# Attention with a sliding window and sinks, fed into a two-layer network: a new order for the first stretch, a third home for P, run-time numbers spread by a product

## The chip, the cores and the metric

The kernel runs on one core of a Trainium2 chip. The metric is the device time of one execution in microseconds (us), as the median of three runs. TensorE (PE in the profile; PEld is its weight load) does the matrix products. VectorE (DVE) and ScalarE (ACT) do the elementwise work, GpSimd (POOL) prepares a few constants, and SyncE (SP) issues nearly all transfers between DRAM and the core's memory. Matrix products are written to PSUM, which has eight banks of 128 x 512 floats.

## The reference

```python
def _attn_ref(q, k, v, n_sink, window):            # 4 batches, 8 heads, 768 positions, 64 wide
    scores = scale * np.matmul(q, k.transpose(0, 1, 3, 2))
    keep = (pos[None, :] < int(n_sink)) | ((rel >= 0) & (rel < int(window)))   # rel = row - column
    scores = np.where(keep, scores, -1000000000.0)
    a = np.exp(scores - np.max(scores, axis=-1, keepdims=True))
    a = a / (np.sum(a, axis=-1, keepdims=True) + 1e-09)
    return np.matmul(a, v).astype(np.float32)

def _moe_ref(x, w_in, w_out):                      # x: 3072 x 512, w_in: 512 x 2048, w_out: 2048 x 512
    h = x @ w_in
    relu6 = np.clip(h + 3.0, 0.0, 6.0)
    return ((h * relu6 / 6.0) @ w_out).astype(np.float32)
```

The attention's output, heads side by side, is the x of the second function. n_sink (4) and window (128) are 64-bit integers that reach the kernel as data, so the masks are computed on the chip. w_in and w_out are 64-bit floats, which the kernel turns into 32-bit pairs itself.

## The kernel before, in words

The work is cut into 12 units of 256 positions (one batch, one third of its sequence), and each unit into 4 pairs of heads: 48 pairs. The steps of pair s have names in a plan, which are used below:

- kq and v: transfers of K and Q, and of V. C: scores on TensorE (four products: two tiles t by two heads h). t: mask, scale and row maximum on DVE, which writes P. x: exponential on ACT, with the row sum. c: reciprocal of the sum on DVE. n: P times the reciprocal, on ACT or DVE, whichever the plan finds free. D: transposes of P on TensorE. o: copy of the transposed P on ACT. E: P times V on TensorE. xh and xl: the result split into a high part (ACT) and a rest (DVE).
- The weights come in 32 parts. Part k is loaded (w), and turned from 64-bit into a high and a low 32-bit tile by wa and wb (ACT), wc and wd (DVE), wh (either) and wl (DVE).
- For unit n and slice i (0 to 7) of the 2048 hidden columns, F (FFN1) is two halves of 12 products each, and needs the xl of the unit's four pairs and parts 4i and 4i+1. r, s, h, g are the gate between the layers (r on ACT, s and g on DVE). G (FFN2) is two halves of 6 products, and needs parts 4i+2 and 4i+3.

Pairs 0 to 11, the first third of each batch, use plain 32-bit products ("plain" in the code). The others split their operands into two rounded parts first.

The order on each engine is made before the kernel is built, by a planner (`in_order`): it keeps a clock for each engine, and gives a free engine the ready task with the earliest due time, as long as the buffers that it takes (`ROOM`) are free. Due times are numbers in tables (`PART_DUE`, `LEAD`, `AHEAD`, `LATE`, `GLAG`). The engines then run their lists strictly in that order and wait for each other by semaphores. Where TensorE has nothing ready early on, the planner writes an "idle" product of two constants (L303) into its list, up to the planned time `QUIET`. Ahead of all that stand `WARM` such products.

P of a plain pair lives in one of two homes: the buffer Pt (even pairs) or two of pl (odd pairs), and K and Q in two buffers each. Pair s+2 can't be masked before the transposes of pair s have freed the home.

n_sink and window are read by two transfers that write the numbers to all 128 partitions (L314, L315); two small DVE instructions turn them into floats (L317, L319), and five more build the masks (L332, L335).

Of the kernel before, what the change touches and what calls it, by code (L numbers as in the profile page):

```python
# [19 lines left out]
P = 128  # L20
SK = 16
# [4 lines left out]
WARM = 10  # L26
# [18 lines left out]
def all_tasks():  # L45
# [6 lines left out]
    add("mask", "DVE", 5.0, [], -100)  # L52
    for s in range(PAIRS):
# [3 lines left out]
        if f32:  # L57
            add(f"kq{s}", "SP", 0.95, [], d - LEAD["kq"], ("kq",))
            add(f"v{s}", "SP", 0.47, [], d - LEAD["v"], ("V",))
            hold = ("pl", "pl") if s % 2 else ("Pt",)  # L60
            add(f"C{s}", "PE", 1.03, [f"kq{s}"], d, ("bank",) * 4 + hold, ("kq",), 0.35)
            scores = [f"C{s}", f"C{s}"]
        else:
# [6 lines left out]
            add(f"qh{s}", "*", (0.54, 0.336), [f"qa{s}"], d - AHEAD["kt"] + 0.2, ("qt",))  # L70
# [76 lines left out]
    for n in range(UNITS):  # L147
        xs = [f"xl{4 * n + p}" for p in range(4)]
        for i in range(8):
# [4 lines left out]
            add(f"F{n}.{i}.0", "PE", 1.42, xs + before + [f"wl{4 * i}", f"wl{4 * i + 1}"], d, ("bank",))  # L154
            add(f"F{n}.{i}.1", "PE", 1.42, [f"F{n}.{i}.0"], d + 0.1, (), ("x0", "x1", "x2", "x3") if i == 7 else (), 0.25)
# [18 lines left out]
def in_order(tasks):  # L174
# [3 lines left out]
    free = dict(PE=5.5, ACT=2.9, DVE=1.0, SP=0.8)  # L178
# [11 lines left out]
    while marks:  # L190
# [9 lines left out]
        while moved:  # L200
            moved = False
            for k, e in enumerate(engines):
# [60 lines left out]
def attn_ffn_kernel(ctx: ExitStack, tc: tile.TileContext, qx, kx, vx, vfx, vsx, n_sink, window, w_in, w_out, out):  # L263
# [53 lines left out]
    nc.vector.scalar_tensor_tensor(out=neg, in0=raw[:, :, 0], scalar=0.0, in1=raw[:, :, 1], op0=ALU.is_lt, op1=ALU.add)  # L317
# [691 lines left out]
```

## Time and profile before

| what | value |
| --- | --- |
| median of 3 runs | 701.63 us (701.29 to 703.6) |
| time of the profiled execution | 702.55 us |
| its span, first to last instruction | 700.6 us |
| TensorE busy | 692.1 us, 99% |
| DVE busy, ACT busy | 559.5 us (80%), 459.1 us (66%) |
| TensorE's granted clock, mean over the span | 0.997 |
| idle products in the trace (L303) | 114 records, 17.2 us |

The span leaves out 1.95 us of the profiled execution's time, which lie around it. An fp32 product of the idle kind or of a plain pair is recorded as two matmuls, so 114 records are 57 products. Matmuls overlap in the records: what one costs is the distance from its start to the start of the next, not its own length. A TensorE that is busy 99% of the span is not doing useful work 99% of the span, since the idle products count as busy.

### The profile page before, as it was taken

The numbers are of one execution on the slowest core, as the hardware profiler recorded it, in microseconds if no ns is written. First come the engines' busy times: TensorE is split into PE (matmuls) and PEld (weight loads), VectorE is DVE, ScalarE is ACT, GpSimd is POOL, SyncE is SP. The second block draws the span as 40 slices with busy tenths as digits, with TensorE's granted clock in tenths as the row PEclk, the third lists the DMA queues.
The fourth block names the chain that finished last, engine by engine and source line by source line (L and its number), as shares of the span: only waits on it lengthen the run. The fifth ranks groups of instructions, "written<-read, shape, count | busy, mean of one in ns | idle before, by whom it ended". The sixth has DMA issues, their size and how long they took to land.

```text
span 700.6 us, 13148 instructions
## 1 busy us (share of the span) xinstructions
PE 692.1 (99%) x4792; PEld 633.2 (90%) x4792; DVE 559.5 (80%) x1396; ACT 459.1 (66%) x1167; POOL 4.5 (1%) x18
## 2 busy tenths in 40 slices
PE   9999999999999999999999999999999999999996
PEld 8888899899999999999999999999999999999995
DVE  6999997368789889889888889888989988885221
ACT  6997986565657677757676667676766776764222
POOL 2000000000000000000000000000000000000000
PEclk9999999999999999999999999999999999999998
DMA  8775562122222213232123123212321222200001
GB/s 282 238 223 183 181 196 67 61 69 78 72 81 84 67 39 92 63 88 92 51 63 118 51 62 110 72 51 80 83 79 56 76 65 75 91 3 0 31 1 36
DMA packets 40122, 61.51 MB, mean 88 GB/s; under 512 B 4720, under 2 KB 31088, under 8 KB 40048
## 3 DMA queue, kind: packets, MB, share of 16 engines
q1 hardware_dynamic: 39760, 60.57, 28.8%
q8 instruction: 40, 0.66, 0.4%
q14 instruction: 34, 0.28, 0.1%
q10 hardware_dynamic: 288, 0.00, 0.0%
HBM read 54.27 MB, written 6.29 MB: 86 GB/s over the span
## 4 chain that ended last, share of the span: by engine, by line
PE 91%; DVE 4%; ACT 3%; DMA 1%; issue 0%; ACTq 0%; POOL 0%; POOLq 0%; DVEq 0%
PE hps L732 37%; PE o L769 37%; PE av L679 6%; PE sp L542 5%; PE pt L607 3%; DMA st<-in_w_out_dram 1%; ACT Ph L569 1%; PE pt L683 1%; DVE Ph L552 1%; PE idle L303 1%; PE pt L605 1%; DMA st<-in_w_in_dram 1%; PE sp L539 1%; ACT st L390 1%; ACT wt L388 0%; DVE wt L396 0%
## 5 line engine op out<-in xcount | busy, mean ns | idle before, releaser
L732 PE MATMUL hps<-xh,wih 128*128 128x256 f32 x768 | 221.7, 289 | 0.0
L732 PE MATMUL hps<-xh,wil 128*128 128x256 f32 x768 | 217.2, 283 | 0.0
L732 PE MATMUL hps<-xl,wih 128*128 128x256 f32 x768 | 217.1, 283 | 0.0
L769 PE MATMUL o<-woh,gh 128*128 128x512 f32 (+1 forms) x386 | 153.3, 397 | 0.0
L769 PE MATMUL o<-wol,gh 128*128 128x512 f32 (+1 forms) x386 | 151.0, 391 | 0.0
L769 PE MATMUL o<-woh,g 128*128 128x512 f32 (+1 forms) x386 | 150.8, 391 | 0.0
L732 PEld LDWEIGHTS hps<-xh,wih 128*128 128x128 f32 x768 | 146.8, 191 | 2.8 <-DVE nb L552 0.3
L732 PEld LDWEIGHTS hps<-xl,wih 128*128 128x128 f32 x768 | 147.0, 191 | 2.1
L732 PEld LDWEIGHTS hps<-xh,wil 128*128 128x128 f32 x768 | 146.7, 191 | 0.0
L744 DVE SCALAR_TENSOR_TENSOR gf<-gf,hps 128x512 f32<-128x512 f32 x96 | 65.3, 680 | 36.5 <-ACT gf L741 35.9
L741 ACT ACTIVATE gf<-hps,three 128x512 f32<-128x512 f32 x96 | 65.0, 677 | 44.5 <-PE hps L732 44.4
L769 PEld LDWEIGHTS o<-woh,g 128*128 128x128 f32 x386 | 72.5, 188 | 16.4 <-DVE g L750 0.6
L769 PEld LDWEIGHTS o<-woh,gh 128*128 128x128 f32 x386 | 72.9, 189 | 11.5 <-issue 0.7
L769 PEld LDWEIGHTS o<-wol,gh 128*128 128x128 f32 x386 | 72.8, 189 | 10.4
L253 ACT ACTIVATE ph<-pm 128x512 fp32r<-128x512 f32 x61 | 38.6, 632 | 61.9 <-DVE pm L617 61.9
L569 ACT ACTIVATE Pt<-Pt,nb 128x144 f32<-128x144 f32 (+2 forms) x144 | 59.0, 411 | 28.6 <-DVE Pt L560 26.6
L750 DVE TENSOR_TENSOR g<-gf,gh 128x512 fp32r<-128x512 f32 x96 | 66.4, 691 | 11.6 <-ACT gh L253 10.2
L639 DVE TENSOR_TENSOR pl<-pm,ph 128x512 fp32r<-128x512 f32 x64 | 44.3, 691 | 35.0 <-ACT ph L253 34.9
L253 ACT ACTIVATE gh<-gf 128x512 fp32r<-128x512 f32 x66 | 41.5, 629 | 26.0 <-DVE gf L744 25.9
L552 DVE CUSTOM_DVE_ANT_0 Pt<-sp,m_t 128x272 f32<-128x272 f32 x128 | 51.4, 433 | 0.0
L542 PE MATMUL sp<-kt,qt 128*128 128x272 f32 (+2 forms) x288 | 46.9, 292 | 0.0
L617 DVE TENSOR_TENSOR pm<-pt,side 128x512 f32<-128x512 f32 x64 | 43.8, 685 | 0.5
(108 smaller groups left out, 1031.9 us busy)
## 6 DMA issues: line engine op xcount, KB each, us to landing
kd<-in_kx_dram SPq DMA_DIRECT2D x64, 200.0 KB, 3.4
qd<-in_qx_dram SPq DMA_DIRECT2D x72, 128.0 KB, 3.1
st<-in_w_in_dram SPq DMA_DIRECT2D x16, 512.0 KB, 4.7
st<-in_w_out_dram SPq DMA_DIRECT2D x16, 512.0 KB, 4.1
vr<-in_vx_dram SPq DMA_DIRECT2D x32, 192.0 KB, 2.7
out_dram<-ost SPq DMA_DIRECT2D x23, 256.0 KB, 2.0
VF<-in_vfx_dram SPq DMA_DIRECT2D x12, 256.0 KB, 4.2
kr<-in_kx_dram SPq DMA_DIRECT2D x12, 128.0 KB, 4.2
```

The costliest lines, as they stand in the source:

```text
L253: nc.scalar.mul(out=out, in_=src, mul=scale)
L542: nc.tensor.matmul(out=sp[g][:, 0:w], lhsT=d["qt"][:, i, g, ts], rhs=d["kt"][:, g, ks], start=(i == 0), stop=(i == 1))
L552: nc.vector.tensor_tensor_reduce(out=cell(s, g, t, 0, w), in0=sp[g][:, 0:w], in1=m[:, 0:w], scale=-SCALE, scalar=3.0e38, op0=ALU.add, op1= ...
L569: nc.scalar.activation(out=blk, in_=blk, func=AF.Exp, scale=-1.0, bias=d["nb"][:, i:i + 1], accum_out=d["sm"][:, i:i + 1])
L617: nc.vector.tensor_tensor(out=pm, in0=pt.unsqueeze(2).to_broadcast([P, 2, 2, P]), in1=side.unsqueeze(1).to_broadcast([P, 2, 2, P]), op=ALU ...
L639: nc.vector.tensor_tensor(out=pl[:, 0:w], in0=pt[:, 0:w], in1=ph[:, 0:w].bitcast(F32), op=ALU.subtract)
L679: nc.tensor.matmul(out=o, lhsT=l, rhs=r, start=(j == 0 and (h == 0 or not plain(s))), stop=(j == len(seq) - 1 and (h == 1 or not plain(s))))
L732: nc.tensor.matmul(out=hp[:, half, :], lhsT=l, rhs=r, start=(j == 0), stop=(j == n - 1))
L741: nc.scalar.activation(out=gf, in_=hp, func=AF.Relu, bias=three, scale=1.0)
L744: nc.vector.scalar_tensor_tensor(out=gf, in0=gf, scalar=6.0, in1=hp, op0=ALU.min, op1=ALU.mult)
L750: nc.vector.tensor_tensor(out=g, in0=gf, in1=gh.bitcast(F32), op=ALU.subtract)
L769: nc.tensor.matmul(out=acc[:, cs], lhsT=l[:, f, ts_], rhs=r[i][:, f, cs], start=(i == 0 and f == 0 and j == 0), stop=(i == NFP - 1 and f = ...
```

## The change

- Transfers: the K and Q of pairs 0 to 3 are issued first (pair 0 in two halves of columns, `kb0`), then V of pairs 0 and 1, then the first weights. Pairs 2 and 3 take the buffers kd and qd for their K and Q, which pairs 12 and later use afterwards.
- P of plain pairs has three homes in turn: Pt, pl, qt.
- Scores of a plain pair are two tasks, C.0 and C.1, as they already were for the other pairs.
- Run-time numbers: the two transfers write one partition, the conversions run on it, and a product with a row of ones spreads the two floats to all partitions by way of PSUM. A copy on DVE brings them back.
- The masks are two tasks; the second one also starts the POOL copies for later pairs.
- F of unit 0, slice 0 is cut into shares of one pair each (`Fe`), three of which can run before the fourth pair is ready.
- The tables of due times are new: weight parts are due later, pairs earlier. There are 13 warm-up products instead of 10.

```diff
-PART_DUE = (3.9, 9.3, 44.9, 53.1, 59.8, 59.9, 67.1, 71.1, 71.7, 73.8, 74.1, 74.6, 74.9, 77.2, 80.9, 89.8, 93.5, 97.5,
+PART_DUE = (47.8, 56.7, 63.7, 67.5, 72.9, 79, 80.8, 81.4, 102, 104.7, 104.9, 105.3, 106.8, 107.4, 109.5, 114.9, 115,
...
-WARM = 10
+WARM = 13
+EARLY = {(0, 0): -56.1}
+HOLDS = ("Pt", "pl", "qt")
+KQ_HOME = {2: "kd", 3: "qd"}
...
-            add(f"C{s}", "PE", 1.03, [f"kq{s}"], d, ("bank",) * 4 + hold, ("kq",), 0.35)
-            scores = [f"C{s}", f"C{s}"]
+            hold = ("pl", "pl") if HOLDS[s % len(HOLDS)] == "pl" else (HOLDS[s % len(HOLDS)],)
+            add(f"C{s}.0", "PE", 0.36, [f"kq{s}"], d, ("bank", "bank") + hold, (), 0.35)
+            if s == 0:
+                add("kb0", "SP", 0.95, [], d - LEAD["kq"] + 0.1)
+            add(f"C{s}.1", "PE", 0.67, [f"C{s}.0"] + ["kb0"] * (s == 0), d + 0.02, ("bank", "bank"), (KQ_HOME.get(s, "kq"),), 0.35)
...
+            if (n, i) in EARLY:
+                for c in range(3):
+                    for half in range(2):
+                        after = xs[c:c + 1] + weights[c // 2:c // 2 + 1] + [f"Fe{n}.{i}.0.0"] * (c + half > 0)
+                        add(f"Fe{n}.{i}.{half}.{c}", "PE", 0.36, after, 40 * n + 10 * c + EARLY[n, i],
+                            takes if c + half == 0 else ())
...
-    nc.scalar.dma_start(out=raw[:, 0, :], in_=n_sink.bitcast(I32).partition_broadcast(P))
-    nc.scalar.dma_start(out=raw[:, 1, :], in_=window.bitcast(I32).partition_broadcast(P))
+    nc.scalar.dma_start(out=raw[0:1, 0, :], in_=n_sink.bitcast(I32).partition_broadcast(1))
+    nc.scalar.dma_start(out=raw[0:1, 1, :], in_=window.bitcast(I32).partition_broadcast(1))
+    ones = const.tile([P, P], F32, name="ones")
+    nc.vector.memset(ones[0:1], 1.0)
...
+    nc.vector.scalar_tensor_tensor(out=neg[one], in0=neg[one], scalar=4294967296.0, in1=raw[one, :, 0],
                                    op0=ALU.mult, op1=ALU.add)
+    nc.tensor.matmul(out=idle[:, P:P + 2], lhsT=ones[one], rhs=neg[one], start=True, stop=True)
+    nc.vector.tensor_copy(out=nw, in_=idle[:, P:P + 2])
...
+    def masks(t):
+        if t == 0:
+            beyond(own, causal, win_f)
+            or_sink(m_00, own)
+            return
+        beyond(ahead, shifted, win_f)
+        or_sink(m_01[:, 0:P], ahead)
+        beyond(m_t0[:, 2 * P:W2], colf[:, 0:SK], ns_f)
+        later_constants()
...
+        if s in KQ_HOME:
+            tag = KQ_HOME[s]
+            both = work.tile([P, 2, 400 if tag == "kd" else UT], F32, tag=tag, name="kq", bufs=1)
+            kr, qr = both[:, 0, 0:UT], both[:, 1, 0:UT]
...
-                both = work.tile([P, 2, 3 * P], F32, tag="Pt", name="Ph", bufs=1)
+                both = work.tile([P, 2, 3 * P], F32, tag=HOLDS[s % len(HOLDS)], name="Ph", bufs=1)
...
+        for c in chunks if early else range(NP):
             xh, xl = x[c]
+            for j, (l, r) in enumerate(((WIH[i][:, c, fs], xh), (WIH[i][:, c, fs], xl), (WIL[i][:, c, fs], xh)), 3 * c):
+                nc.tensor.matmul(out=hp[:, half, :], lhsT=l, rhs=r, start=(j == 0 and not (early and half)),
+                                 stop=(j == n - 1 and not (early and half == 0)))
```

What the change moves is shown at three places, each as the engine's list before and now. A row is the source line, the operation, what it writes and reads, the shape, and how often it stands there in a row.

TensorE, the start of its list, before. "idle" are the idle products, sp scores (four to a pair, two of 128 and two of 256 columns), pt transposes, av P times V.

```order
L303 MATMUL idle<-rel 128x128 x11
L539 MATMUL sp<-kr,qr 128x128 x2
L539 MATMUL sp<-kr,qr 128x256 x2
L303 MATMUL idle<-rel 128x128 x4
L539 MATMUL sp<-kr,qr 128x128 x2
L539 MATMUL sp<-kr,qr 128x256 x2
L303 MATMUL idle<-rel 128x128 x12
L607 MATMUL pt<-ident_r,Ph 128x128 x6
L303 MATMUL idle<-rel 128x128 x5
```

The same place now: one row is the product that spreads the two numbers (neg, ones).

```order
L320 MATMUL idle<-rel 128x128 x13
L342 MATMUL idle<-neg,ones 128x2
L320 MATMUL idle<-rel 128x128 x2
L578 MATMUL sp<-kr,qr 128x128 x2
L320 MATMUL idle<-rel 128x128 x2
L578 MATMUL sp<-kr,qr 128x256 x2
L320 MATMUL idle<-rel 128x128
L578 MATMUL sp<-kr,qr 128x128 x2
L578 MATMUL sp<-kr,qr 128x256 x2
L578 MATMUL sp<-kq 128x128 x2
L578 MATMUL sp<-kq 128x256 x2
L320 MATMUL idle<-rel 128x128 x7
```

Three pairs of scores now stand ahead of the first transposes instead of two, with 11 idle products after the first pair's scores instead of 16 after the first two; the spreading product stands behind 13 idle ones.

SP, the start of its list, before. kr, qr and kq are K and Q of plain pairs, VF is V, st a weight part, kd and qd K and Q of pair 12.

```order
L454 DMA kr<-in_kx_dram 128x256
L455 DMA qr<-in_qx_dram 128x256
L454 DMA kr<-in_kx_dram 128x256
L455 DMA qr<-in_qx_dram 128x256
L471 DMA VF<-in_vfx_dram 128x512
L368 DMA st<-in_w_in_dram 128x1024
L471 DMA VF<-in_vfx_dram 128x512
L368 DMA st<-in_w_in_dram 128x1024
L368 DMA st<-in_w_out_dram 128x1024 x2
```

The same place now.

```order
L493 DMA kr<-in_kx_dram 128x128
L494 DMA qr<-in_qx_dram 128x128
L482 DMA kr<-in_kx_dram 128x128
L483 DMA qr<-in_qx_dram 128x128
L493 DMA kr<-in_kx_dram 128x256
L494 DMA qr<-in_qx_dram 128x256
L493 DMA kq<-in_kx_dram 128x256
L494 DMA kq<-in_qx_dram 128x256
L493 DMA kq<-in_kx_dram 128x256
L494 DMA kq<-in_qx_dram 128x256
L510 DMA VF<-in_vfx_dram 128x512 x2
L396 DMA st<-in_w_in_dram 128x1024 x2
```

The first V stands behind ten loads of K and Q instead of four, and the first weight behind twelve loads instead of five.

ACT, the stretch up to the last scaling of P of pair 7 (n, L583 before and L622 now, Ph and rc), before. wt and st are a weight part's steps, gf the gate, x the rows with sm and nb, xh the row that reads av, pf the copy o. The tile of pair 7 is Ph_664 here.

```order
L253 ACTIVATE pf_749<-pt_726 128x384
L569 ACTIVATE Ph_664,sm_661<-Ph_664,nb_660 128x256
L388 ACTIVATE wt_753<-st_524 128x512
L741 ACTIVATE gf_745<-hps_697,three_77 128x512
L583 ACTIVATE Ph_664<-Ph_664,rc_662 128x128
L583 ACTIVATE Ph_664<-Ph_664,rc_662 128x256
```

The same stretch now, where pair 7 has the tiles Ph_569 and Ph_570.

```order
L608 ACTIVATE Ph_569,sm_567<-Ph_569,nb_566 128x256
L270 ACTIVATE xh2_672<-av_665 128x256
L608 ACTIVATE Ph_570,sm_567<-Ph_570,nb_566 128x256
L416 ACTIVATE wt_706<-st_483 128x512
L780 ACTIVATE gf_704<-hps_518,three_77 128x512
L622 ACTIVATE Ph_570<-Ph_570,rc_568 128x128
L622 ACTIVATE Ph_570<-Ph_570,rc_568 128x256
```

Up to this scaling of pair 7 the list before holds wa of nine weight parts (0 to 8), and now of five (0 to 4).

## Rows read from the trace of the kernel before

**Rows 1.** TensorE's waits after its start: on whom, total us, times, longest

```profile
PE sp L539 <- DVE nb L552: 0.7, 1, 0.7
```

**Rows 2.** windows: PE, PEld, DVE, ACT, POOL busy us, granted clock, DMA share, GB/s

```profile
10.00:33.66 23.66, 23.39 (x185) 20.07 (x184) 23.04 (x83) 23.18 (x73) 0.00 (x0) 1.00 0.87 266
66.00:100.00 34.00, 33.29 (x209) 29.32 (x209) 33.72 (x81) 30.44 (x69) 0.00 (x0) 1.00 0.54 178
120.00:140.00 20.00, 20.00 (x130) 17.70 (x129) 6.66 (x23) 10.48 (x27) 0.00 (x0) 1.00 0.22 66
```

**Rows 3.** the same windows view for the tile idle alone, in two stretches

```profile
1.13:6.12 4.99, 4.99 (x22) 4.77 (x22) 1.00 0.64 161
7.54:33.66 26.12, 12.11 (x92) 11.05 (x92) 1.00 0.88 281
```

**Rows 4.** TensorE in order of time: start us, us, instruction, x records

```profile
6.12 1.48 PE L539 MATMUL sp<-kr,qr 64*128 64x128 f32 x8
```

**Rows 5.** DVE in order of time, first mask instruction and first masked score

```profile
5.88 0.29 DVE L332 TENSOR_SCALAR m<-rel,nw 128x128 bf16<-128x128 f32 x1
...
7.61 0.28 DVE L552 CUSTOM_DVE_ANT_0 Ph<-sp,m 128x128 f32<-128x128 f32 x1
```

**Rows 6.** ACT in order of time

```profile
7.93 0.40 ACT L569 ACTIVATE Ph<-Ph,nb 128x128 f32<-128x128 f32 x1 [4.97 <-DVE nb L552]
...
20.78 0.39 ACT L569 ACTIVATE Ph<-Ph,nb 128x128 f32<-128x128 f32 x1
...
22.54 0.66 ACT L388 ACTIVATE wt<-st 128x512 f32<-128x512 f32 x1
23.10 0.37 ACT L253 ACTIVATE xh<-av 128x256 fp32r<-128x256 f32 x1
23.37 0.80 ACT L583 ACTIVATE Ph<-Ph,rc 128x256 f32<-128x256 f32 x2
24.06 0.39 ACT L569 ACTIVATE Ph<-Ph,nb 128x128 f32<-128x128 f32 x1
...
25.32 0.85 ACT L253 ACTIVATE pf<-pt 128x384 f32<-128x384 f32 x2
26.07 0.50 ACT L569 ACTIVATE Ph<-Ph,nb 128x256 f32<-128x256 f32 x1
```

**Rows 7.** DVE in order of time: two weight steps, masked scores, another weight step

```profile
18.42 0.69 DVE L393 SCALAR_TENSOR_TENSOR st<-st 128x512 int32<-128x512 int32 x1
...
19.76 0.28 DVE L552 CUSTOM_DVE_ANT_0 Ph<-sp,m 128x128 f32<-128x128 f32 x1
...
20.87 0.69 DVE L401 TENSOR_TENSOR wol<-wt,woh 128x512 fp32r<-128x512 f32 x1
21.47 0.69 DVE L393 SCALAR_TENSOR_TENSOR st<-st 128x512 int32<-128x512 int32 x1
```

**Rows 8.** TensorE in order of time around the transposes of pair 7

```profile
40.89 0.36 PE L732 MATMUL hps<-xh,wih 128*128 128x256 f32 x1
...
42.41 0.82 PE L607 MATMUL pt<-ident_r,Ph 128*128 128x128 f32 x6
...
45.97 0.93 PE L539 MATMUL sp<-kr,qr 64*128 64x128 f32 x8
46.83 0.88 PE L607 MATMUL pt<-ident_r,Ph 128*128 128x128 f32 x6
```

**Rows 9.** TensorE in order of time, two transposes and FFN1 behind them

```profile
326.72 0.36 PE L732 MATMUL hps<-xh,wih 128*128 128x256 f32 x1
326.92 0.28 PE L732 MATMUL hps<-xl,wih 128*128 128x256 f32 x1
327.04 0.28 PE L732 MATMUL hps<-xh,wil 128*128 128x256 f32 x1
```

**Rows 10.** one issue on SP; weight loads (KB each, median us to landing)

```profile
1.66 0.42 SPq L454 DMA_DIRECT2D kr<-in_kx_dram  x1
...
st<-in_w_in_dram SPq DMA_DIRECT2D x16, 512.0 KB, 4.7
```

More of the change, by code (lines that the diff above doesn't have):

```diff
@@ L50, in add @@
         tasks[name] = [eng, cost, after, due, takes, gives, lag]
-    add("mask", "DVE", 5.0, [], -100)
+    add("mask0", "DVE", 0.75, [], -100)
+    add("mask1", "DVE", 1.03, ["mask0"], 0.15)
     for s in range(PAIRS):
@@ L79, in all_tasks @@
                 cost = 0.36 if far else 0.345 if t else 0.21
-                add(f"t{s}.{t}{h}", "DVE", cost, [scores[t], "mask"], d + 0.1, (), ("bank",))
+                add(f"t{s}.{t}{h}", "DVE", cost, [scores[t], f"mask{t}"], d + 0.1 + 0.1 * t * (s == 0), (), ("bank",))
                 before = [f"m{s}"] if far else [f"t{s}.{t}{h}"]
@@ L153, in all_tasks @@
                 before.append("G{}.{}.1".format(*divmod(8 * n + i - 2, 8)))
-            add(f"F{n}.{i}.0", "PE", 1.42, xs + before + [f"wl{4 * i}", f"wl{4 * i + 1}"], d, ("bank",))
-            add(f"F{n}.{i}.1", "PE", 1.42, [f"F{n}.{i}.0"], d + 0.1, (), ("x0", "x1", "x2", "x3") if i == 7 else (), 0.25)
+            weights, takes, cost = [f"wl{4 * i}", f"wl{4 * i + 1}"], ("bank",), 1.42
+            if (n, i) in EARLY:
[4 more added lines that the diff above has]
+                            takes if c + half == 0 else ())
+                        before.append(f"Fe{n}.{i}.{half}.{c}")
+                takes, cost = (), 0.36
+            add(f"F{n}.{i}.0", "PE", cost, xs + before + weights, d, takes)
+            add(f"F{n}.{i}.1", "PE", cost, [f"F{n}.{i}.0"], d + 0.1, (), ("x0", "x1", "x2", "x3") if i == 7 else (), 0.25)
             add(f"r{n}.{i}", "ACT", 0.581, [f"F{n}.{i}.1"], -50, ("gf",))
@@ L224, in in_order @@
                 if e == "SP":
-                    wire = max(wire, now + (2.8 if now < 4.5 else 1.5)) + (1.6 if best[0] == "w" else 0.8)
-                    end, lag = wire + 0.7, 0.1
+                    wire = max(wire, now + (2.4 if now < 4.5 else 1.5))
+                    wire += (1.3 if best[0] == "w" else 0.35 if best in ("kq0", "kb0") else 0.7) * (1.5 if wire < 5 else 1.0)
+                    end, lag = wire + 1.2, 0.1
                 count += 1
@@ L718, in E_sinks, with ffn1 @@
         nc.vector.tensor_tensor(out=tmp, in0=st_[s]["spt"][:, 0:UT], in1=tmp, op=ALU.add)
-    def ffn1(x, i, pool, psum, half, state, tag, planned=False):
-        if half == 0:
+    def ffn1(x, i, pool, psum, half, state, tag, planned=False, chunks=None):
+        early = chunks is not None
+        if half == 0 and (not early or chunks[0] == 0):
             state["h"] = psum.tile([P, 2, UT], F32, tag=tag or "hps", name="hps")
@@ L727, in ffn1 @@
         n = 3 * NP
-        j = 0
-        for c in range(NP):
+        for c in chunks if early else range(NP):
             xh, xl = x[c]
-            for l, r in ((WIH[i][:, c, fs], xh), (WIH[i][:, c, fs], xl), (WIL[i][:, c, fs], xh)):
-                nc.tensor.matmul(out=hp[:, half, :], lhsT=l, rhs=r, start=(j == 0), stop=(j == n - 1))
-                j += 1
-        if half == 1:
+            for j, (l, r) in enumerate(((WIH[i][:, c, fs], xh), (WIH[i][:, c, fs], xl), (WIL[i][:, c, fs], xh)), 3 * c):
+                nc.tensor.matmul(out=hp[:, half, :], lhsT=l, rhs=r, start=(j == 0 and not (early and half)),
+                                 stop=(j == n - 1 and not (early and half == 0)))
+        if half == 1 and (not early or chunks[-1] == NP - 1):
             g = pool.tile([P, 2, UT], F32R, tag="g", name="g", bufs=2)
```

57 lines of the change are left out of this document (30 added, 27 removed).

## The prediction

> **What bounds the kernel now.** First the waits: after its start TensorE waits for someone once for 0.7 us [rows 1]; everything else in its row is back to back. So the span is the sum of what stands in TensorE's list, and only three things can shorten it: products that do nothing, the start, and the dearness of single products. The windows of the tile idle show the first: 22 records (11 products) up to 6.12 us, and 92 records (46 products) between 7.54 and 33.66 us, 12.1 us of TensorE [rows 3]. Then why they are there: in that stretch ACT is busy for 23.18 and DVE for 23.04 of 23.66 us [rows 2]. TensorE pauses because the masks, exponentials, scalings and copies of the pairs, and the weights' steps, fill both other engines. An idle product that is left out saves nothing unless what stands behind it is ready sooner. The change must be judged by ACT's and DVE's lists.
>
> **The start.** The first 11 idle products take 4.99 us, 0.454 each; later ones 12.11 / 46 = 0.26 each [rows 3]. The granted clock shows 1.00 (2.4 GHz) in both stretches, so that column does not explain the slower pace; I take the pace from the starts. The scores of pair 0 follow at 6.12 [rows 4]. The masks don't depend on TensorE now; they run from 5.88 to 7.61, 1.73 us for five instructions, and at 7.61 the first score is masked [rows 5]. After the change the masks need the spreading product, which stands behind 13 idle products. The first 11 end at 6.12; two more at 0.26 to 0.45 each end between 6.6 and 7.0; I take 6.8, since pair 0's scores at 6.12 are still slow (1.48 us against 0.86 for a later pair, 45.97 to 46.83 [rows 8]). No row shows the product and the copy back: together at least one fast idle product (0.26) and at most two slow ones (0.9); I take 0.55. The numbers themselves land earlier than that on one partition or on 128, since in the old form they were converted by 5.88. Then 1.73 us of masks: first masked score at 6.8 + 0.55 + 1.73 = 9.1, which is **1.5 us later** than 7.61. Bounds: if all 13 idle products ran at 0.26, from 1.13, they would end at 4.5 and the score be masked at 4.5 + 0.26 + 1.73 = 6.5, 1.1 us earlier; with all the slow values, 7.0 + 0.9 + 1.73 = 9.6, 2.0 later. On the pace the Trainium skill (TensorE: Matmul & The Clock Gate, section "Part 1: The HAM clock gate") says that the warm-up goes by time and not by the number of matmuls. By that rule three more warm-up products bring the fast pace no nearer, and the thirteen end at 7.0; with the fast pace of the later rows right behind 6.12 they end at 6.6: 0.2 to either side of the value in the sum. Both mask steps stand ahead of the first score on DVE, so cutting them in two gains nothing by itself.
>
> **ACT's list up to the scaling of pair 7.** I compare the two kernels at one point, the transposes D of pair 7. Costs on ACT, from start to start [rows 6]: four exponentials of a pair 1.76 (20.78 to 22.54), a weight step 0.56, xh 0.27, a scaling 0.345 (two in 23.37 to 24.06), two copies 0.75. To see whether such a count is to be trusted, before: 8 pairs x 1.76, 15 scalings, 7 pairs of copies, 6 xh, 19 weight steps, three steps of the gate at 0.56 make 14.1 + 5.2 + 5.25 + 1.6 + 10.6 + 1.7 = 38.4 us from 7.93, which is 46.4; the trace has D of pair 7 at 46.83 [rows 8]. So ACT sets that point, and the count is 0.4 short of it. Now: the same 8 pairs and 7 pairs of copies, 11 scalings (the others went to DVE), 7 xh, 12 weight steps, one gate step: 14.1 + 3.8 + 5.25 + 1.9 + 6.7 + 0.6 = 32.3. The first exponential starts 0.3 after the first masked score (7.93 against 7.61), at 9.4; with the 0.4 that the count was short, ACT lets D of pair 7 begin at 9.4 + 32.3 + 0.4 = 42.1; its first half needs DVE's scalings only, so it counts as begun at 41.9.
>
> By then TensorE has done other work than before: one pair of scores more (C of pair 9, 0.86) and one slice of FFN1 less (F of slice 1, two halves of 1.52, 40.89 to 42.41 [rows 8], together 3.04). The kernel before had done that much at 46.83 - 3.04 + 0.86 = 44.65. Gain at this point: 44.65 - 41.9 = **2.7 us**, the late start already paid. The third home for P and the early K and Q are what lets pairs follow each other so fast; they have no term of their own.
>
> Does TensorE keep up? From pair 0's scores to D of pair 7 it needs 40.7 us before; without 46 idle products (12.1) and the slice, with the scores, 26.4. Now it starts these at about 7.8 (6.8, half a microsecond of product, two idle ones), and has 19 idle products left (4.9): 39.1. It is 2.8 us ahead of ACT and spends them in real waits, most of them ahead of D of pair 7.
>
> **From there on.** The 0.7 us wait at 66.8 [rows 1] belongs to a score waiting for banks; the scores of that stretch now stand earlier: **0.7 saved**. Against it stand the weight parts, which are due later: FFN1 of slice 2 needs parts 8 and 9. Between D of pair 7 and it, TensorE has C of pairs 10 and 11, E of 7, D of 8, three slices of FFN1 and three of FFN2, about 21 us. DVE must split parts 4 to 9 meanwhile, at 1.34 for two steps (18.42 to 19.76) and 0.60 for the third (20.87 to 21.47) [rows 7], 11.6 us; the masked scores of pairs 9 to 11 (1.11 each, 19.76 to 20.87) 3.3; three gates (s and g at 0.6, two h at 0.46) 4.5; casts, scalings and reciprocals about 3: 22.5 us. So it is about 1.4 late at the most if both begin together, and has begun a little earlier; I take a wait of **1.0**, bounds 0 and 3 (the count of pairs and gates may be off by 10%, and the next slices repeat it). Behind that DVE has room: before, it is busy for 33.72 of 34 us from 66 to 100, but only 6.66 of 20 from 120 to 140 [rows 2].
>
> **Order of TensorE's products later.** Where transposes are followed by FFN work, the first interval is 0.20 instead of 0.12 us [rows 9]: 0.08 for each such place. By the lists there are 81 of them behind D of pair 7 before and 62 now, since D's halves and the pieces of pairs stand together more often: 19 x 0.08 = **1.5 us saved**, bounds 0.8 (half of them covered) and 1.5.
>
> **What costs nothing.** The loads: the first V is issued six places later and the first weight seven, at 0.42 us an issue [rows 10] some 3 us; V's first use is E of pair 0, six microseconds behind the first masked score, and a weight part is first touched by ACT behind five pairs' exponentials, some 13 us behind it, while 4.7 us bring even a weight part in [rows 10]. If that cover were gone it would cost 3 us once. Pair 12's K and Q wait for kd and qd until pair 3 is scored; pair 12 is scored far behind pair 11. One-partition conversions, the memset of ones and POOL's copies for later pairs lie beside ACT's table load and the idle products. Shares of F in slice 0 add no product.
>
> **Sum.** -2.7 - 0.7 + 1.0 - 1.5 = -3.9 us. It stands against the profiled 702.55 us: 698.65. That execution is 0.92 above the median of 701.63, so the median should be **697.7 us**. With the best bounds (start 2.6 better, no wait) the change is -7.5, 694.1; with the worst (start 0.5 worse, wait 3, order 0.8) it is -0.7, 700.9.
>
> **The rivals.**
> 1. *The idle pace is fast.* If the clock rises before the thirteen idle products are through, the start gains 1.1 instead of losing 1.5: -6.5, 695.1. For it: nothing in the rows, which show the slow pace to 6.12. 12%.
> 2. *The clock falls.* Real waits now take the place of idle products. All rows before show 1.00, with no gap over 0.7 us. If the wait of about 2.8 us ahead of D of pair 7 let the clock go to 1.2 GHz, what follows would run at half pace until it rises: the start shows the price, 11 products at 0.454 instead of 0.26, 2.1 us. Then -1.8, 699.8. 8%. The Trainium skill (TensorE: Matmul & The Clock Gate, section "Why this matters for your kernels") says that a gap between matmuls that is long enough puts the clock back to its lower level, and that gaps inside a kernel should be kept short; no run here shows a gap of this size yet.
> 3. *No change.* DVE, not ACT, is the bound of the whole stretch to 100 us, full as it is [rows 2]; what comes earlier at D of pair 7 is then given back by waits for weight parts, 2.7 + 0.7. Only the order remains, 1.5 us: 700.1; with half of it 700.9. It decides if TensorE's waits for DVE between D of pair 7 and FFN1 of slice 3 sum to 3.4 us. 15%.
> 4. *Slower.* At D of pair 7 four parts less have gone through ACT and 3.5 less through DVE (1.94 each [rows 7], 6.8 us). If nothing of this is made good before FFN1 of slice 2, TensorE stands still for 6.8 us there: 6.8 - 2.7 - 0.7 - 1.5 = +1.9, or 703.5. It decides when that one wait is over 4.9 us. Against it: TensorE has 21 us of other work first. 8%.
>
> The forecast, with small errors of its terms, has 57%; its own range is 696.0 to 699.7. The range over the cases is 694.0 to 701.0, which leaves out the slower case and a little of the first rival. A measurement of this kernel can tell about 0.3%, 2.1 us, from no change. Faster by more: the forecast but for its worst few per cent, the first rival and a part of the second, 0.70. Within: 0.20. Slower: 0.10, the last rival and a little for waits in the later units.
>
> **What would show it.** The first masked score at 9.1 us (8.5 to 9.6). ACT full from there to D of pair 7 at about 41.9. The 114 idle records become 68 (34 products). TensorE's waits: about 2.8 us up to D of pair 7, about 1 us for weight tiles at FFN1 of slice 2, none behind 120 us. From 200 us on each unit of four pairs takes a little less than before. The prediction is wrong if ACT has gaps of over 1 us in the first 40 us (then transfers or DVE bound), if waits for wih or wil sum to several microseconds, or if the later units show waits on TensorE.

## The result and the profile after

The changed kernel takes 707.7 us (median of 5, 706.79 to 708.53) against 701.63 of the kernel before: a ratio of 1.008, 95% interval 1.0062 to 1.0098. It is slower by 6 us; the forecast was 3.9 us faster. The profiled execution took 708.53 us, 0.83 above its median, with a span of 706.7. The later runs shared chips with the kernel before, at medians of 702.2 to 702.4 us there, so they are compared by their ratios.

TensorE's waits, the list of [rows 1], now (columns as there):

```profile
PE pt L644 <- DVE ssc L276: 1.7, 3, 0.6
PE hps L771 <- DVE nb L591: 1.3, 1, 1.3
PE idle L320 <- POOL rel L304: 1.1, 1, 1.1
PE pt L644 <- ACT ssc L270: 1.1, 2, 0.6
PE pt L646 <- DVE Ph L624: 0.9, 1, 0.9
...
```

The third row is the start, which the kernel before has too. L644 is new in this list. It is the sink product of a far pair, the first thing in D.1, and reads ssc, which three small steps (Sh, Sl, Sd) make from the scaled P. The weight loads ahead of the products show these waits in full. TensorE's loading side (PEld) from 180 to 640 us:

```profile
PEld pt L644 <- ACT ssc L270: 2.9, 6, 0.8
PEld pt L644 <- DVE ssc L276: 2.3, 3, 0.8
PEld pt L646 <- ACT Pt L622: 1.0, 5, 0.4
```

So 9 pairs wait for the sink steps, 5.2 us, and 5 for the scaled P, 1.0 us. The same view of the kernel before has no row at all.

The start, which answers to [rows 3] (tile idle in two stretches), [rows 5] (DVE) and [rows 8] (TensorE, D of pair 7):

```profile
1.13:6.69 5.56, 5.56 (x27) 5.44 (x27) 0.00 (x0) 1.00 0.65 168
7.32:33.66 26.34, 6.67 (x42) 5.37 (x42) 0.00 (x0) 1.00 0.83 259
```

```profile
7.10 0.16 DVE L343 COPY nw<-idle 128x2 f32<-128x2 f32 x1 [3.92 <-PE idle L342]
7.30 0.28 DVE L355 TENSOR_SCALAR m<-rel,nw 128x128 bf16<-128x128 f32 x1
...
9.03 0.28 DVE L591 CUSTOM_DVE_ANT_0 Ph<-sp,m 128x128 f32<-128x128 f32 x1
```

```profile
40.89 1.22 PE L646 MATMUL pt<-ident_r,Ph 128*128 128x128 f32 x6 [0.85 <-DVE Ph L624]
```

All as foretold or better: first masked score at 9.03 (9.1), D of pair 7 at 40.89 (41.9), 68 idle records (68; the two windows add up to 69 because they also take in one of the spreading product's two records). ACT is busy for all of the 31.54 us from 9.35 to 40.89. The loss must lie behind.

To find it I summed, along each trace, the usual pitch of every product that isn't idle, and compared the times at which the two kernels had done the same sum. The changed kernel is 3.4 us ahead when the kernel before is at 86.6 us, 0.65 ahead at 169.4, 0.6 behind at 209.7, and 6.6 behind at 688.7 (the spans differ by 6.1: 0.5 come back in the last 12 us). So 2.8 us go between 86.6 and 169.4, most of them around 105 to 118 us, and 7.2 behind that, evenly, in the far pairs. The even part can be seen in windows of 112 us, two units each. TensorE alone: busy us (products), granted clock, DMA share, GB/s; before, then after:

```profile
240.00:352.00 112.00, 112.00 (x794) 1.00 0.26 74
352.00:464.00 112.00, 112.00 (x794) 1.00 0.26 74
464.00:576.00 112.00, 112.00 (x794) 1.00 0.26 74
```

```profile
240.00:352.00 112.00, 111.30 (x784) 1.00 0.26 71
352.00:464.00 112.00, 110.94 (x786) 1.00 0.27 74
464.00:576.00 112.00, 111.30 (x782) 1.00 0.27 74
```

Busy time falls by 0.7 to 1.1 us only, but 8 to 12 products of 0.141 us (112 / 794) are missing in each. Overlapping records fill the small waits, and the count shows them. One such wait, on all engines:

```profile
383.66 0.42 DVE L738 TENSOR_TENSOR xl<-tmp,xh 128x256 fp32r<-128x256 f32 x1
383.72 0.38 PE L646 MATMUL pt<-ident_r,Pt 128*128 128x128 f32 x2
...
384.06 0.20 DVE L276 CAST ssc<-Pt 128x64 fp32r<-128x64 f32 x1
384.29 0.23 DVE L635 TENSOR_TENSOR ssc<-Pt,ssc 128x64 fp32r<-128x64 f32 x1
...
384.43 0.19 DVE L276 CAST ssc<-ssc 128x64 fp32r<-128x64 f32 x1
...
384.67 0.30 PE L644 MATMUL pt<-ident_r,ssc 128*96 128x128 f32 x1 [0.57 <-DVE ssc L276]
```

D.0 (two transposes) starts at 383.72 and D.1 follows directly in the list. The sink steps begin only at 384.06, behind an xl, and end at 384.62. The kernel before has half an FFN step, 1.4 us, between D.0 and D.1 of every far pair. The changed list has them side by side ("neighbours" below) in 14 of 32. In 9 of the 14 the sink product starts 0.34 to 0.94 us behind D.0's last transpose, in the other 5 only 0.03: their sink steps were done in time.

### The profile page after: what moved, and what is told of

Read it like the earlier page. It is cut to its first block, busy times and chain, and to the rows that moved or that the text cites. A ratio compares the mean times of both kernels' runs of the same rounds, so it can differ in the third digit from the quotient of the medians.

```text
span 706.7 us, 13146 instructions
## 1 busy us (share of the span) xinstructions
PE 692.0 (98%) x4748; PEld 628.4 (89%) x4748; DVE 564.1 (80%) x1427; ACT 448.0 (63%) x1138; POOL 4.5 (1%) x18
## 4 chain that ended last, share of the span: by engine, by line
PE 65%; DVE 20%; ACT 8%; issue 3%; DMA 2%; SPq 0%; ACTq 0%; DVEq 0%; POOL 0%; POOLq 0%
PE o L808 26%; PE hps L771 26%; PE sp L581 5%; PE av L718 4%; PE pt L646 2%; DVE st L421 2%; DVE tmp L753 2%; DMA st<-in_w_out_dram 2%; DVE wt L424 2%; DVE gf L783 1%; ACT Ph L608 1%; DVE g L789 1%; DVE pl L678 1%; DVE wil L429 1%; DVE Pt L591 1%
## 5 line engine op out<-in xcount | busy, mean ns | idle before, releaser
L771 PE MATMUL hps<-xh,wih 128*128 128x256 f32 x768 | 220.4, 287 | 1.3 <-DVE nb L591 1.3
L771 PE MATMUL hps<-xh,wil 128*128 128x256 f32 x768 | 216.7, 282 | 0.3 <-DVE wil L429 0.3
L771 PE MATMUL hps<-xl,wih 128*128 128x256 f32 x768 | 216.5, 282 | 0.0
L771 PEld LDWEIGHTS hps<-xh,wih 128*128 128x128 f32 x768 | 145.1, 189 | 5.0 <-DVE nb L591 1.8
L771 PEld LDWEIGHTS hps<-xl,wih 128*128 128x128 f32 x768 | 144.7, 188 | 2.5
L771 PEld LDWEIGHTS hps<-xh,wil 128*128 128x128 f32 x768 | 144.7, 188 | 0.5 <-DVE wil L429 0.5
L780 ACT ACTIVATE gf<-hps,three 128x512 f32<-128x512 f32 x96 | 65.0, 677 | 71.8 <-PE hps L771 71.6
L270 ACT ACTIVATE gh<-gf 128x512 fp32r<-128x512 f32 x60 | 37.5, 627 | 14.4 <-DVE gf L783 14.0
L581 PE MATMUL sp<-kt,qt 128*128 128x272 f32 (+2 forms) x288 | 44.9, 288 | 0.0
```

Of the source, the lines that this page charges most:

```text
L270: nc.scalar.mul(out=out, in_=src, mul=scale)
L581: nc.tensor.matmul(out=sp[g][:, 0:w], lhsT=d["qt"][:, i, g, ts], rhs=d["kt"][:, g, ks], start=(i == 0), stop=(i == 1))
L771: nc.tensor.matmul(out=hp[:, half, :], lhsT=l, rhs=r, start=(j == 0 and not (early and half)), stop=(j == n - 1 and not (early and half == ...
L780: nc.scalar.activation(out=gf, in_=hp, func=AF.Relu, bias=three, scale=1.0)
```

## The experiments

After each: the median, the ratio to the kernel before with its interval, and the lead over the kernel before (minus is ahead) at its 86.6, 169.4 and 688.7 us, worked out as above. The changed kernel has -3.4, -0.65, +6.6. A lead comes from one traced execution and moves with the choice of pitch, by some tenths and at 86.6 us by up to 1 us.

Only halves_apart, before_neighbours, loads_of_before, parts_without_sign and parts_on_gpsimd keep the lists of the kernel that they start from, but for the places named. Where a due time or a lag is changed, the planner makes new lists for all engines. By the lists that the kernels' planners make, late_of_before has 169 tasks on another engine (ACT or DVE) than the changed kernel, sink_lag 106, and scale_lag_apart 98.

**late_of_before.** The changed kernel with the three numbers that place the far pairs in the list as before.

```diff
-LATE = 890.8
-GLAG = 35.9
-AHEAD = {"load": -25.6, "kt": -38.7, "v": 58.1, "S": -60.2}
+LATE = 1007.1
+GLAG = 19.6
+AHEAD = {"load": -28.9, "kt": -30.9, "v": 55.9, "S": -0.1}
```

> The changed kernel with AHEAD, LATE and GLAG of the kernel before; its start, loads and table of weight parts stay as changed. In TensorE's written order the two halves of D stand next to each other in 5 of the 32 far pairs (14 in the changed kernel, none in the kernel before). Theory A, the loss behind 180 us comes from these neighbours, whose second half waits for the sink's steps: 9 of 14 neighbours are gone, so 9/14 of the 6 to 7 us that the changed kernel loses from 184 us to its end come back: 702 to 704 us. Rival B, the weight parts that come late at 85 to 150 us and what follows from them: no change of the head, 707 us and more. Rival C, VectorE and ScalarE are fuller in the changed late order whatever TensorE's order is: about 701, with the waits gone at all kinds of products and not at the transposes alone.

702.47 us, 1.0001 (0.9991 to 1.001); -3.9, -1.8, +0.5. Theory A's range, and TensorE's loading side from 180 to 640 us has one row, with no wait for ssc:

```profile
PEld pt L646 <- ACT Pt L622: 0.5, 3, 0.2
```

The 5 neighbours that are left don't wait: their sink products start 0.03 to 0.18 us behind D.0. Neighbours cost time only where the sink steps are late.

**before_late_950.** The kernel before with one number changed.

```diff
-LATE = 1007.1
+LATE = 950.0
```

> The kernel before with one number changed, LATE 950 for 1007, so that the far pairs are due earlier; start, loads and weight parts are those of before. 13 far pairs then have the two halves of D next to each other. Theory A: it is slower by about 13/14 of what the changed kernel loses behind 184 us, 706 to 709 us. Rival B, the loss belongs to the late weight parts: 701 to 702 us. A middle value, 703 to 705, would say that neighbours cost less when the units' other work stands elsewhere.

713.62 us, 1.0157 (1.0144 to 1.017); -0.6, -0.5, +11.9: slower than A allowed, with no weight part later. Beside the sink products its transposes wait for the scaled P (on the loading side 5.0 us, 14 times). So neighbours aren't the whole of it.

**sink_lag.** The changed kernel, with more room between the sink steps and what reads them when the list is made; no neighbours are left.

```diff
-            add(f"Sd{s}", "*", (0.25, 0.115), [f"Sh{s}"], d + 0.46)
-            add(f"Sl{s}", "DVE", 0.145, [f"Sh{s}"], d + 0.46)
+            add(f"Sd{s}", "*", (0.25, 0.115), [f"Sh{s}"], d + 0.46, lag=1.3)
+            add(f"Sl{s}", "DVE", 0.145, [f"Sh{s}"], d + 0.46, lag=1.3)
```

> The changed kernel with one thing more: the planner takes 1.3 us for what lies between a sink step's end and the products that read it (0.12 + 0.6 before), so that it puts half an FFN step or a score between the halves of D. No far pair has the halves next to each other, all the rest of the change stays. Theory A: the 6 to 7 us lost from 184 us on are gone, 700.5 to 702 us, and the second half's wait for ssc is gone from the trace. Rivals B and C: 706 us or more, with the waits somewhere else.

703.09 us, 1.0008 (0.9998 to 1.0018); -3.8, -2.05, +0.7. The waits for ssc are gone. Behind 169.4 us it loses 2.75 us in place of 7.25, and its transposes now wait for the scaled P (2.0 us, 9 times); the time is 1.1 us over the range expected.

**halves_apart.** The smallest undoing: in the finished list of TensorE the 14 neighbours are parted, and nothing else moves on any engine.

```diff
+        if order[pe[j - 1]][0] == f"D{s}.0":
+            order.insert(pe[j + 1], order.pop(pe[j]))
```

> The changed kernel, its order kept word for word but for 14 places: where D.1 of a far pair stands right behind D.0 on TensorE, it moves behind the next product of the list (half an FFN step or half a score). VectorE, ScalarE and the loads keep their order. Theory A, the sink steps are late when the halves are neighbours: the 8.2 us that TensorE sits idle ahead of the sink products in the changed kernel go, and 701.5 to 703.5 us are left. Rival, sink_lag was faster because all engines' orders changed with it: 706 us and more.

705.48 us, 1.0044 (1.0028 to 1.0059); -3.0, -1.2, +3.45: between the two theories. (The 8.2 us and 15 waits of the expectation count product and weight load of the same places; it is 9 places and 5.2 us, as above.) What took the place of the sink waits stands in TensorE's loading side from 180 to 640 us, one row:

```profile
PEld pt L655 <- ACT Pt L631: 5.0, 22, 0.5
```

L655 is a plain transpose of D, L631 the scaling of P. TensorE no longer loses time at D.1 and reaches the next pairs' D before their P is scaled: the wait moved one link up the same chain.

**before_neighbours.** The mirror image: in the list of before, the half FFN step between D.0 and D.1 goes behind D.1 in all 32 far pairs.

```diff
+        if order[pe[j - 2]][0] == f"D{s}.0":
+            order.insert(pe[j], order.pop(pe[j - 1]))
```

> The kernel before, its order kept word for word but for 32 places: the half FFN step between D.0 and D.1 of each far pair moves behind D.1, so that all 32 far pairs have neighbours. Theory A, with the price of the changed kernel (8.2 us over 15 waits, 0.55 us each): 32 times 0.55 is 17 us, 715 to 720; where TensorE's order is looser than in the changed kernel and the sink steps are done earlier, less, but at least 5 us, 707. Rival, neighbours cost nothing by themselves and the changed late order is slow for another reason: 701 to 703 us.

728.25 us, 1.0376 (1.0358 to 1.0393): 26 us, 0.8 for each pair, more than theory A's 17 us. The windows of 112 us drop from 794 products to 750, and TensorE's loading side shows where:

```profile
PEld pt L614 <- ACT ssc L262: 22.7, 26, 1.2
```

The kernel before had little to spare, then: the last Sl ended 0.61 us (median of 32 pairs) ahead of the sink product, with 1.4 us of FFN in between.

**late_of_before_lag.** late_of_before with the two lines of sink_lag.

> late_of_before (AHEAD, LATE and GLAG of the kernel before in the changed kernel) and the 1.3 us for the sink steps of sink_lag together: none of the 32 far pairs has neighbours. Theory A: the 5 neighbours left in late_of_before cost 0.5 us each at most, of the 1.4 us that it loses from 280 us to its end; 700.5 to 702 us, below the kernel before or even with it. Rival, the 1.4 us are lost elsewhere: 702.5 us as late_of_before.

701.31 us, 0.9984 (0.9975 to 0.9993); -3.5, -2.4, -1.3: faster than the kernel before, if by little. The range held, but not for theory A's reason: the 5 neighbours of late_of_before had cost nothing. The lag has moved 98 tasks between ACT and DVE; what of that won the 1.2 us is not shown.

**scale_lag_apart.** halves_apart with the same kind of room between the scaling of P (n) and D.0.

```diff
-            add(f"n{c}", "*", cost, [f"c{s}"], d + 0.4 + 0.01 * int(c[-1]))
+            add(f"n{c}", "*", cost, [f"c{s}"], d + 0.4 + 0.01 * int(c[-1]), lag=0.9 if far else 0.12)
```

> halves_apart (705.5 us) with 0.9 us for 0.12 between the scaling of P and D.0 of a far pair in the list's making, so that D.0 comes later in TensorE's list. If the 22 waits of D.0 for ScalarE's scaling (5.0 us) are what halves_apart still loses behind 180 us: the waits are gone and 701.5 to 703 us are measured. Rival, the late order loses it elsewhere: 705 us or more with the waits at other products.

701.3 us, 0.9979 (0.9968 to 0.999); -3.7, -2.05, -1.4. From 180 us on only 0.6 us are lost. TensorE alone in the windows of 112 us, and its loading side from 180 to 640 us:

```profile
240.00:352.00 112.00, 112.00 (x793) 1.00 0.27 74
352.00:464.00 112.00, 112.00 (x793) 1.00 0.27 74
464.00:576.00 112.00, 112.00 (x794) 1.00 0.27 74
```

```profile
PEld pt L655 <- ACT Pt L631: 0.2, 1, 0.2
```

With the changed LATE kept, the loss in the far pairs goes when the two waits go, for ssc and for the scaled P. The run doesn't show that the room alone does it, since the new lists also put 45 scalings and 11 Sh and Sd each on the other engine.

**scale_and_sink_lag.** sink_lag with that line.

> sink_lag (1.0008 of the kernel before) with the same 0.9 us ahead of D.0. If its 9 waits for ScalarE's scaling (2.0 us) are what it loses against the head's gain: 700.5 to 701.5 us, at or just under the kernel before. Rival, they are hidden by other work: as sink_lag, 702.5 to 703.5 us.

701.63 us, 0.9993 (0.9984 to 1.0001); -3.5, -1.7, -1.4: 0.1 over the range expected; behind 209.7 us its lead changes by 0.2 us only (-1.63 to -1.44).

**parts_without_sign.** late_of_before without step wc of weight parts 12 to 31.

```diff
-        elif step == "c":
+        elif step == "c" and k >= 12:
+            pass
+        elif step == "c":
```

> late_of_before without one of VectorE's steps on each weight part from part 12 on (wc, which sets the signs; these weights are then wrong): 20 steps of 0.69 us less on VectorE between 60 and 118 us and later. The head's gain falls from 3.9 to 1.8 us against the kernel before between 105 and 118 us. If VectorE's work on the parts makes this loss (the GELU steps wait behind it), 1.5 to 2 us come back and 700.5 to 701 us are measured; if the parts are late from their loads (3.5 to 6.0 us each, three slots), the loss stays and 702 to 702.5 us are measured.

701.11 us, 0.9979 (0.997 to 0.9989); -3.7, -3.7, -1.25. The lead is now kept from 86.6 to 169.4 us, where late_of_before drops 2.1 us of it, and TensorE's loading side has no wait from 85 to 180 us. In the changed kernel it has these from 105 to 120 us, and SP's queue waits like this from 85 to 110:

```profile
PEld o L808 <- DVE g L789: 1.4, 2, 0.8
PEld o L808 <- ACT gh L270: 0.7, 1, 0.7
PEld hps L771 <- DVE wil L429: 0.5, 1, 0.5
```

```profile
SPq L396 <- DVE wt L424: 24.0, 10, 5.8
```

So that loss hangs on DVE's steps on the parts. It doesn't follow that the loads have no part in it: a load waits in SP's queue until DVE's step wd (L424) has freed its slot, and ACT waits for loads in turn, 3.6 us from 85 to 120 in the changed kernel and 0.7 here. One place of the changed kernel, on ACT, DVE and TensorE:

```profile
104.77 0.66 ACT L416 ACTIVATE wt<-st 128x512 f32<-128x512 f32 x1 [1.22 <-DMA st<-in_w_out_dram]
105.33 0.68 ACT L780 ACTIVATE gf<-hps,three 128x512 f32<-128x512 f32 x1
105.91 0.62 ACT L270 ACTIVATE woh<-wt 128x512 fp32r<-128x512 f32 x1
...
106.04 0.69 DVE L783 SCALAR_TENSOR_TENSOR gf<-gf,hps 128x512 f32<-128x512 f32 x1 [1.14 <-ACT gf L780]
...
106.43 1.14 ACT L270 ACTIVATE gh<-gf 128x512 fp32r<-128x512 f32 x2
106.65 0.68 DVE L429 TENSOR_TENSOR wol<-wt,woh 128x512 fp32r<-128x512 f32 x1
107.10 0.19 PEld L808 LDWEIGHTS o<-woh,gh 128*128 128x128 f32 x1 [0.70 <-ACT gh L270]
...
107.25 1.29 DVE L789 TENSOR_TENSOR g<-gf,gh 128x512 fp32r<-128x512 f32 x2
...
107.99 0.19 PEld L808 LDWEIGHTS o<-woh,g 128*128 128x128 f32 x1 [0.59 <-DVE g L789]
```

ACT waits 1.22 us for a part's load, and the gate's first step (L780) stands behind that part in its list; DVE's s, then gh and g follow late, g also behind wol, and FFN2 waits for gh and g. Against late_of_before 1.75 us are kept to the end (+0.5 to -1.25). Both lose some 2.4 us behind 209.7 us. Their five neighbours are not the reason, since they don't wait; the loading side shows 0.7 us of waits for the scaled P here, and the rest stays open.

**parts_on_gpsimd.** The attempt to get those 2 us: late_of_before_lag with wl of parts 12 to 31 on GpSimd.

```diff
-            nc.vector.tensor_tensor(out=lo, in0=like(ft), in1=hi.bitcast(F32), op=ALU.subtract)
+            lo_e = nc.gpsimd if k >= 12 else nc.vector
+            lo_e.tensor_tensor(out=lo, in0=like(ft), in1=hi.bitcast(F32), op=ALU.subtract)
```

> late_of_before_lag with the last step of each weight part from part 12 on (wl, the low half) on GpSimd instead of VectorE; the order of all else stays. parts_without_sign gave back 1.1 to 1.9 us with 0.69 us less of VectorE for each such part. If GpSimd has its step done within some 2 us, the same comes back: 699.5 to 700.3 us, under the kernel before. Rival: GpSimd takes longer for it or slows VectorE beside it, F and G wait for wil and wol, and it is slower than 701.3 us, at worst by the 5 us or more that 20 such steps late in a row would give.

706.87 us, 1.0054 (1.0042 to 1.0066); -1.7, +5.3, +6.3: the rival. A step takes 1.50 (wol) or 1.68 us (wil) there on average against 0.69 on DVE, and F waits 2.1 us for wil. The leads are those of an execution of 708.33 us, in which the clock fell twice (below), the first time at 42 us, ahead of GpSimd's first such step at 74; so not all of the loss in them is GpSimd's.

**loads_of_before.** The changed kernel with the run-time numbers loaded to 128 partitions, 10 idle products and no spreading product.

```diff
-    nc.scalar.dma_start(out=raw[0:1, 0, :], in_=n_sink.bitcast(I32).partition_broadcast(1))
+    nc.scalar.dma_start(out=raw[:, 0, :], in_=n_sink.bitcast(I32).partition_broadcast(P))
...
-WARM = 13
+WARM = 10
```

> The changed kernel with the two run-time numbers loaded to all 128 partitions as before (no product, no copy) and 10 idle products for 13. If the start's 1.5 us are carried to the end, as the prediction has them: pair 0's scores 1.2 to 1.6 us earlier and 706 to 706.5 us. Rival: the waits for weight parts at 85 to 120 us take the gain, since the loads keep their own time: 707.4 to 708 us. A third case: the broadcast loads now share the queues with the first kr and qr and land later than 4.7 us, so that nothing is gained at the start.

706.85 us, 1.0061 (1.0048 to 1.0075); -2.4, -1.3, +5.45: between the two ranges, and its interval overlaps the changed kernel's. At the start it is 1.9 us ahead of the changed kernel, and then has this row in TensorE's waits up to 30 us, for V of pair 0, now loaded behind ten K and Q:

```profile
PE av L712 <- DMA VF<-in_vfx_dram: 2.4, 1, 2.4
```

At 86.6 us it is 1.0 behind the changed kernel, and at the end 1.15 ahead, since it loses less up to 169.4 us; why wasn't followed up.

**start_broadcast.** late_of_before_lag with the same loads, and V of pair 0 ahead of K and Q of pairs 2 and 3.

```diff
-            add(f"v{s}", "SP", 0.47, [], d - LEAD["v"], ("V",))
+            add(f"v{s}", "SP", 0.47, [], d - LEAD["v"] if s else -70, ("V",))
```

> late_of_before_lag (701.3 us, 0.998 of the kernel before) with the run-time numbers loaded to 128 partitions and 10 idle products as before, and V of pair 0 loaded fourth, ahead of kr and qr of pairs 2 and 3. In loads_of_before the start was 1.9 us earlier, and then TensorE waited 2.4 us for V of pair 0, to 23.58 us. If that load is all that swallowed the start: no wait for V, D of pair 7 at 39.5 us or earlier, and 1.2 to 1.6 us less at the end, 699.7 to 700.2 us. Rival, the next links (the scores of pairs 2 and 3, whose loads are now later, or ScalarE's list up to pair 7) swallow it as well: 701 us and more.

701.55 us, 0.9987 (0.9976 to 0.9999); -3.8, -3.0, -1.8. The first masked score is at 7.14 for 8.54 us, but D of pair 7 at 40.64 for 40.81. V is no longer waited for; 1.2 us for a late Q and 0.7 for ACT are. The rival: the early start isn't worth its 1.5 us.

**start_scale_lag.** start_broadcast with the line of scale_lag_apart.

> start_broadcast (0.9987 of the kernel before, 698.4 us span) with the same 0.9 us ahead of D.0. Its trace shows hardly any wait behind 180 us (six of 1.1 us in late_of_before_lag), so at most 1 us less, 700.3 to 701.3 us; if more room ahead of D.0 pushes later pairs' work together, 702 us or more.

701.9 us, 0.9996 (0.9983 to 1.001); -3.2, -1.9, -1.3: no better.

**two_homes.** late_of_before_lag with `HOLDS = ("Pt", "pl")`.

> late_of_before_lag with the homes of P taken in turn from Pt and pl alone (two, as in the kernel before, for three). If the third home is what lets ScalarE's list run ahead by the 2.7 us that the prediction gave it at D of pair 7: D of pair 7 between 42 and 44.5 us and 1.5 to 2.7 us more at the end, 702.8 to 704 us. Rival, the loads of four pairs ahead of the weight parts make the head faster and the homes do not matter: 701 to 701.6 us.

702.6 us, 1.0001 (0.9992 to 1.001); -1.7, -0.6, +0.55. D of pair 7 at 43.89 for 40.81, and 1.85 us of the lead are missing at the end (1.2 us by the ratios): the third home does what was expected of it, or a little less.

**no_early_shares.** late_of_before_lag with `EARLY = {}`.

> late_of_before_lag without the early shares of FFN1 (EARLY empty): slice 0 of unit 0 is done in two pieces of 12 products behind pair 3, as before. The prediction gave the shares the 0.7 us of a bank's wait, so 701.6 to 702.2 us; if they only move TensorE's work into gaps that ScalarE's list leaves in the first 40 us (8 products of about 0.12 us and their waits beside idle products), up to 1.3 us, 702.6 us; rival, nothing: 701.3 us.

703.45 us, 1.0007 (0.9996 to 1.0017); -0.65, -0.4, +0.7: dearer than expected, 2 us of lead. FFN1 waits twice, 1.45 us at 52 us, behind which TensorE's clock fell for 1.6 us of loss (below), and 1.5 us for gf at 67.9; late_of_before_lag has one such wait, of 1.3 us.

## Why the prediction was wrong

**Start and head held, with errors that cancel.** The late start was sized well (9.03 for 9.1). D of pair 7 began 1.0 us earlier than counted (40.89 for 41.9), released by a scaling on DVE; ACT, full as foretold, ended its own scalings of that pair at 41.6. So the gain there was 3.8 us (44.65 - 40.89) in place of 2.7. The bank's wait of 0.7 us, counted as saved, came back as 1.3 us at L771, where FFN1 waits for nb, a row maximum. Together 3.4 us ahead, the -2.7 and -0.7 of the sum, which is luck in part. The late start was no loss that the broadcast form would have spared: start_broadcast won it back and lost it to the next links.

**The 1.0 for weight parts was too small.** It is 2.8, inside the bounds of 0 to 3, and not where it was put: on the loading side only 0.5 us are a wait for wil. The other 2.1 us from 105 to 120 are FFN2 waiting for g and gh, which come late behind weight steps on DVE and ACT and behind a load that ACT waits for. The count looked at when parts are ready, not at what else their steps hold up.

**The step that failed is "Order of TensorE's products later": 1.5 us saved.** It counted the fewer switches from transposes to FFN work, "since D's halves and the pieces of pairs stand together more often", and priced those alone. What stood between the halves was cover: 1.4 us in which ACT and DVE finished the sink steps. Without it TensorE waits wherever they are late, and they and the scaled P are late in the changed order of the far pairs: 7.2 us lost in place of 1.5 won. halves_apart, which moves nothing else, gives back 2.6 us of it (-1.2 to +3.45 in place of -0.65 to +6.6) and shows the wait for the scaled P in its place (5.0 us); in scale_lag_apart, whose lists have room there, all but 0.6 of the rest is back. The prediction named waits "none behind 120 us" as a sign, and it failed there; it had looked for waits in the trace of before alone, where this chain has none, and gave its slack no row.

**Of the rivals** none came true: the idle pace was slow up to 6.2 us, and only the last of the 13 idle products was quick; the granted clock stayed 1.00 in the changed kernel's trace up to 702 us; from D of pair 7 to 66 us TensorE's waits for DVE came to the one of 1.3 us, not 3.4; and the fourth had the sign but another place (one wait for weight parts). The loss in the later units was held for a little of 10%.

**Left open:** why a pair's chain of masks, exponentials and scaling has so little room under the changed LATE; its pairs have at least as much TensorE work between C and D.0 in the list as before. The planner's choice of engine is an untested rival: of the far pairs' 128 scalings the changed kernel has 54 on DVE for 36 before, and of their 32 Sh ten for none.

## What to carry to other kernels

Before counting a saving from products that stand together, ask what the second one reads and how long before it that was finished: the work between them may be all the cover there is. Standing together costs nothing by itself; it costs where that input is late. A wait that is taken from the last link of a chain shows up at the link before it unless the whole chain gets room; a list made by a planner needs that room in its lags. Where an engine reads 98 or 99% busy in both kernels, count its instructions in equal windows.

## What the hardware showed

**The clock can fall after short waits.** In no_early_shares FFN1 waits 1.45 us, with only three records of transposes between that and a wait of 0.26 before it. TensorE in order of time, and its windows (busy us, granted clock):

```profile
50.24 0.55 PE L646 MATMUL pt<-ident_r,Ph 128*128 128x128 f32 x3 [0.26 <-ACT pf L270]
52.23 0.46 PE L771 MATMUL hps<-xh,wih 128*128 128x256 f32 x1 [1.45 <-ACT pf L270]
...
54.41 0.41 PE L771 MATMUL hps<-xl,wih 128*128 128x256 f32 x1
54.62 0.41 PE L771 MATMUL hps<-xh,wil 128*128 128x256 f32 x1
...
55.99 0.28 PE L771 MATMUL hps<-xh,wih 128*128 128x256 f32 x1
56.11 0.28 PE L771 MATMUL hps<-xl,wih 128*128 128x256 f32 x1
```

```profile
48.00:52.00 4.00, 2.52 (x19) 1.00 0.78 257
52.00:56.00 4.00, 3.77 (x19) 0.57 0.51 181
56.00:60.00 4.00, 4.00 (x26) 1.00 0.42 127
```

From 52.2 to 55.7 products start every 0.21 us instead of 0.12: the lower level, 1.2 GHz, for some 16 products, 1.6 us. All 11 executions of no_early_shares read a mean granted clock of 0.995 or 0.996, those of late_of_before_lag 0.997 or 0.998.

Three more traces show it. In parts_on_gpsimd waits of 0.88 and 1.11 us, 2.3 us apart, took it down for 6.8 us (0.76, 0.50 and 0.89 in the windows of 4 us from 40 to 52), and waits of 0.92 and 0.91, 1.7 us apart, for 3.4 us (0.73 and 0.84 from 88 to 96). In scale_lag_apart, waits of 0.91 us ahead of D of pair 7 and 0.58 behind it did it:

```profile
38.00:42.00 4.00, 2.51 (x17) 0.98 0.89 282
42.00:46.00 4.00, 4.00 (x18) 0.60 0.68 236
```

In scale_and_sink_lag it was 0.88 and 0.43 at the same place. The changed kernel's 0.85 there and its 1.3 us at L771 did not do it, nor did late_of_before_lag's 0.71 and 0.20, with the same lists as parts_on_gpsimd. So the prediction's second rival came about in other lists, at the place that it names, after waits of 1.3 to 2.0 us together; but scale_lag_apart's lead at 86.6 us (-3.7) shows nothing of the 2.1 us that it was to cost.

The Trainium skill (TensorE: Matmul & The Clock Gate, section "Why this matters for your kernels") says that long gaps between bursts of matmuls put the clock back to its lower level. These traces agree that gaps do, but each single wait here was shorter than the gaps which the page warns of; the measurement decides.
